# Column-normalised attention and a soft mixture of experts: two tiles of each unit split instead of three, five value halves loaded transposed, and a new order of steps and loads

## The chip, the core and the metric

The kernel runs on one NeuronCore of one Trainium2 chip. The metric is the device time of one execution in microseconds. Before the change it is 343.02 us (median of three runs, 342.92 to 343.14). The engines are named as the profile names them: PE (TensorE), DVE (VectorE), ACT (ScalarE), POOL (GpSimd) and SP (SyncE, which issues nearly all DMAs here).

## What is computed

Four batches of q, k and v, each 5056 tokens by 256 channels in fp32. The attention is between channels: a 256 by 256 matrix for each batch.

```python
qn = q / (norm(q, axis=1) + 1e-6);  kn = k / (norm(k, axis=1) + 1e-6)
s  = kn.transpose(0, 2, 1) @ qn / tau          # 256 x 256 per batch
a  = softmax(s, -1)
x  = (v @ a).reshape(4 * 5056, 256)
logits = x @ phi                               # 32 slots
d  = softmax(logits, 0);  slot_in = d.T @ x    # over all 20224 tokens
slot_out[e] = relu(slot_in[e] @ w1[e]) @ w2[e] # 8 experts, 4 slots each
out = softmax(logits, 1) @ slot_out
```

## The kernel before

**Stage one: 40 units.** Tokens of q and k come in units of 512 (four tiles of 128); ten units make a batch (`UB`), so units 0 to 39. `load_qk` brings one unit into a `raw` buffer (four of them, 1 MB each). `score_tiles` adds each tile's part of k-transposed times q to two banks of the accumulator memory, one for each half `m` of k's channels. A tile is treated in one of two ways. A **raw** tile (line 213) is multiplied in plain fp32. A **split** tile (lines 224 and 227) is first divided into a rounded part by ACT (`cast`, line 155) and the remainder by DVE (`low`, line 163), both in the tile `hl`; then one matmul of 512 columns and one of 256 do the work in the rounded type. `n_split` says how many of a unit's four tiles are split: none in unit 0, two up to unit 11, three from unit 12 on. For the column norms ACT squares every unit (`square`, line 181) and DVE adds it up (`add`, lines 194 to 197).

**The border between two batches.** When a batch's last unit is done, `att_join` copies the upper halves of the two score banks to SBUF (ACT, `shi`, line 244) and adds the lower halves (DVE, `ssb`, line 246). The next batch overwrites these banks, so its first score matmul waits for `ssb`. Then come the norms: `att_sums` (PE, `n`, line 253), `att_copy` (ACT, `nsb`, line 264), `att_cols` (PE, `nn`, line 270), `att_pow` (DVE `rn`, then POOL, line 276), `att_norm` (ACT `dg`, line 288), `att_row` (PE, `rq`, line 294); then scaling, exponentials and turns down to the batch's small matrix `M` (`att_phi`, `att_m`).

**Pairs of v.** v comes in pairs of 1024 tokens, five to a batch, pairs 0 to 19. `load_v` brings a pair in natural order (six buffers). For the logits v is needed with channels on the partitions: the first channel half comes from DRAM already transposed (`load_vt`, `vt0`, 0.5 MB a pair), the second is transposed by PE (`turn`, `vTp`, line 368, four transposes for each half pair) and copied out by ACT (`turned`, line 385). `logits` (line 399) then multiplies by `M`; each two or three pairs make a group whose running maximum goes through DVE and two tiny matmuls (`peak_row`, `peak_run`, `shift`: `rp`, `rowrun`, `cp`); `gather` (PE, `G`, line 508) multiplies the exponentials by natural v and, with that, frees the pair's buffer.

**Order.** Nothing schedules this by itself. Each step is entered in a list with a number (`at(key, step, ...)`): unit `u` has the keys around `u`. The list is sorted and emitted, so each engine, SP's queue too, executes strictly in the order of the keys.

**Stage two.** A second list takes over behind unit 39. The unit buffers (`raw`, `hl`, `sq`) are given back and the same memory is cut into seven 1 MB slots `w` and six half MB slots `x`, for the last pairs of v and for the expert weights. In this list the last batch's small chain, the logits of pairs 15 to 19, the gathers 11 to 19 and the exponentials of `combine` (the softmax over slots: DVE `cm`, POOL and ACT `nat`) take turns. The first load in it is the second half of pair 16, whose first half the first list has put at its end; both go to the buffer that `gather` of pair 10 frees.

**Stage three.** The experts (`up`, `H`, line 901; `down`, `O`, line 927), then 20 output pairs (`out_pair`, line 992) of 1 MB each, written to DRAM.

Of the kernel before, what the change touches and what calls it, by code (L numbers as in the profile page):

```python
# [8 lines left out]
F32 = mybir.dt.float32  # L9
F32R = mybir.dt.float32r  # L10
# [13 lines left out]
def colnorm_attention_soft_moe(  # L24
# [9 lines left out]
    vt7: bass.AP,  # L34
    tau: bass.AP,
    phi: bass.AP,
    w1: bass.AP,
    w2: bass.AP,
    sel: bass.AP,
    oa: bass.AP,  # L40
# [50 lines left out]

    def load_vt(p, t=None, slot=None):
        b, i = divmod(p, PB)
        if slot:
            t = slot(f"vt{p}_0")
        if t is None:
            t = tpool.tile([P, 8 * P], F32, tag="vt0", name=f"vt{p}_0", bufs=3)
        if i < PB - 1:
            sp.dma_start(t, vt8[b, i])
        else:  # L100
            sp.dma_start(t[:, : 8 * P - HD], vt7[b])
        vts[p, 0] = t

# [17 lines left out]
    act.activation(warm, ones[:, 0:1], AF.Exp)  # L121
    phi_sb = const.tile([P, 2, S], F32, name="phi_sb")
    rtau = const.tile([P, 1], F32, name="rtau")
    sel_sb = const.tile([P, 2], F32, name="sel_sb")
    act.dma_start(phi_sb, phi.rearrange("(n p) s -> p n s", p=P))
    act.dma_start(rtau, tau.partition_broadcast(P))
    act.dma_start(sel_sb, sel)
    fold = const.tile([P, S], F32, name="fold")
# [150 lines left out]
    def att_norm(b):  # L279
        rn = st[b]["rn"]  # L280
        dve.tensor_scalar_add(rn, rn, 1e-6)
        dve.reciprocal(rn, rn)
        rk = bpool.tile([P, 2], F32, tag="rk", name=f"rk{b}")
        dg = bpool.tile([P, C], F32, tag="dg", name=f"dg{b}")
        if b == 0:
            dve.reciprocal(rtau, rtau)
# [85 lines left out]
    def turned(i, m=1, where=None, eng=None):  # L372
        p, h = divmod(i, 2)
        if h == 0:
            if where:
                where = xslot(f"vt{p}_{m}")
            else:
                where = tpool.tile([P, 8 * P], F32, tag="vt1", name=f"vt{p}_{m}", bufs=2)
            vts[p, m] = where
        x = vts[p, m]  # L380
        tp, n = tps[i, m]
        if eng is dve:
            dve.tensor_copy(x[:, h * UT : h * UT + n], tp[:, :n])
        else:
            act.copy(x[:, h * UT : h * UT + n], tp[:, :n])  # L385
# [233 lines left out]
    for b in range(3):  # L619
        k = UB * (b + 1)  # L620
        at(k - 0.42, att_join, b)
        at(k + 0.20, att_sums, b)
        at(k + 0.45, att_copy, b)
        at(k + 0.55, att_cols, b)
# [165 lines left out]
    at(0.6, last_exp, 0)  # L790
# [297 lines left out]
```

## Time and profile before

| what | value |
|---|---|
| median of three runs | 343.02 us |
| the profiled execution | 344.6 us |
| its span, first to last instruction | 342.8 us |
| PE busy | 278.7 us, 81% |
| DVE busy | 237.5 us, 69% |
| ACT busy | 208.3 us, 61% |
| DMA traffic | 110.36 MB, 322 GB/s on average |

The profile is of one execution. A group's line gives its count, its busy time in us and the mean of one instruction in ns. A row of the timeline gives start and duration in us and, in square brackets, how long the engine stood idle before it and for whom. A row of a stretch gives its length, then the busy time of PE, of PE's weight loads, of DVE, ACT and POOL (with instruction counts), the granted clock of PE as a share of full speed, the busy share of the DMA engines and their GB/s. PE rows overlap: the time between two starts, not the duration of one, is what a matmul costs.

### The profile page before, as it was taken

The page shows a single profiled execution, that of the slowest core. Times are in us where ns is not written, and L with a number is a line of the kernel's source. Part 1 is how long each engine was busy: PE and PEld are TensorE (multiplying, and loading weights), DVE is VectorE, ACT ScalarE, POOL GpSimd, SP SyncE. Part 2 cuts the span into 40 slices and gives each one's busy share as a digit, 9 for nine tenths or more (in the row PEclk, how much of TensorE's full clock was granted, in tenths as well). Part 3 has the DMA queues.
Part 4 walks back from the last instruction along what each step waited for, and adds up shares of the span by engine and source line. Part 5 has one row for each costly group of instructions (what it writes and reads, how often), then busy time and mean ns, then how long its engine had stood idle before and what let it go on. Part 6 is the DMA issues. An engine that isn't in the chain of part 4 may idle for free. (4 is left out here: it accounts for less than half of the span.)

```text
span 342.8 us, 5518 instructions
## 1 busy us (share of the span) xinstructions
PE 278.7 (81%) x2164; PEld 194.1 (57%) x2164; DVE 237.5 (69%) x340; ACT 208.3 (61%) x281; POOL 27.8 (8%) x18
## 2 busy tenths in 40 slices
PE   4899869899799899999989998839689998898000
PEld 2687638677566778667667675514345355565000
DVE  1399955799996889987879994526755245999000
ACT  1978865799795898787788863514530235677000
POOL 0000002000002000002000001021303231200000
PEclk9999969999999999999999999958785899999655
DMA  5999998799866889987897940999999602999997
GB/s 186 424 382 302 422 414 350 284 354 367 358 228 227 344 302 395 358 306 267 318 386 294 326 168 10 380 399 415 422 413 416 234 2 94 419 402 401 420 403 283
DMA packets 21401, 110.36 MB, mean 322 GB/s; under 512 B 2944, under 2 KB 3200, under 8 KB 12800
## 3 DMA queue, kind: packets, MB, share of 16 engines
q1 hardware_dynamic: 20816, 109.98, 82.9%
q8 instruction: 17, 0.28, 0.3%
q10 hardware_dynamic: 560, 0.03, 0.1%
q14 instruction: 8, 0.07, 0.0%
HBM read 89.29 MB, written 20.71 MB: 321 GB/s over the span
## 5 line engine op out<-in xcount | busy, mean ns | idle before, releaser
L224 PE MATMUL S<-hl 128*128 128x512 f32 x212 | 83.7, 429 | 3.4 <-DVE ssb L246 3.1
L181 ACT ACTIVATE sq<-raw 128x2048 f32<-128x2048 f32 x36 | 69.0, 1916 | 13.9 <-DMA raw<-in_qk_dram 6.6
L163 DVE TENSOR_TENSOR hl<-raw,hl 128x1536 fp32r<-128x1536 f32 (+1 forms) x39 | 62.5, 1603 | 19.2 <-ACT hl L155 18.9
L197 DVE TENSOR_TENSOR sq<-sq,sq 128x2048 f32<-128x2048 f32 (+1 forms) x37 | 73.4, 1983 | 0.0
L213 PE MATMUL S<-raw 128*128 128x256 f32 (+1 forms) x216 | 57.7, 400 | 5.2 <-DMA raw<-in_qk_dram 5.2
L155 ACT CAST hl<-raw 128x1536 fp32r<-128x1536 f32 (+1 forms) x39 | 52.7, 1352 | 13.9 <-issue 8.8
L227 PE MATMUL S<-hl 128*128 128x256 f32 x212 | 59.6, 281 | 0.0
L224 PEld LDWEIGHTS S<-hl 128*128 128x128 f32 x212 | 40.0, 189 | 24.3 <-issue 10.4
L213 PEld LDWEIGHTS S<-raw 128*128 128x128 f32 (+1 forms) x216 | 39.6, 199 | 12.4 <-DMA raw<-in_qk_dram 7.0
L227 PEld LDWEIGHTS S<-hl 128*128 128x128 f32 x212 | 40.3, 190 | 0.4
L385 ACT COPY vt<-vTp 128x512 f32<-128x512 f32 (+1 forms) x40 | 22.9, 582 | 18.3 <-PE vTp L368 18.0
L368 PE MATMUL vTp<-ident,v 128*128 128x128 f32 (+1 forms) x160 | 25.0, 281 | 6.8 <-DMA v<-in_v_dram 6.8
L992 PE MATMUL op<-so,cT 32*128 32x256 f32 x320 | 27.7, 410 | 2.9 <-DVE o L987 1.5
L399 PE MATMUL L<-vt,M 128*32 128x256 f32 (+1 forms) x320 | 25.2, 432 | 2.8 <-ACT M L356 1.3
L985 ACT COPY o<-op 128x512 f32<-128x512 f32 x40 | 21.2, 598 | 8.7 <-PE op L992 5.8
L992 PEld LDWEIGHTS op<-so,cT 32*128 32x128 f32 x320 | 19.7, 183 | 11.0 <-DVE o L987 6.3
L987 DVE COPY o<-op 128x512 f32<-128x512 f32 x40 | 24.2, 672 | 2.4 <-PE op L992 2.4
L508 PE MATMUL G<-v,dn 128*32 128x256 f32 (+1 forms) x320 | 25.3, 400 | 0.0
L276 POOL TENSOR_TENSOR rn<-rn,half 128x4 f32<-128x4 f32 x4 | 8.4, 2107 | 203.3 <-DVE rn L275 102.2
L368 PEld LDWEIGHTS vTp<-ident,v 128*128 128x128 f32 (+1 forms) x160 | 18.5, 142 | 10.9 <-issue 10.0
L399 PEld LDWEIGHTS L<-vt,M 128*32 128x32 f32 x320 | 9.2, 120 | 14.5 <-issue 6.3
L508 PEld LDWEIGHTS G<-v,dn 128*32 128x32 f32 (+1 forms) x320 | 11.8, 114 | 8.8 <-issue 3.9
(124 smaller groups left out, 253.1 us busy)
## 6 DMA issues: line engine op xcount, KB each, us to landing
raw<-in_qk_dram SPq DMA_DIRECT2D x35, 1024.0 KB, 6.4
out_dram<-o SPq DMA_DIRECT2D x16, 1024.0 KB, 11.7
v<-in_v_dram SPq DMA_DIRECT2D x31, 512.0 KB, 6.9
w<-in_moe_w_dram SPq DMA_DIRECT2D x14, 1024.0 KB, 12.4
vt<-in_vt_dram SPq DMA_DIRECT2D x16, 512.0 KB, 8.2
raw<-in_qk_dram SPq DMA_DIRECT2D x4, 768.0 KB, 6.0
out_dram<-o SPq DMA_DIRECT2D x4, 768.0 KB, 13.7
v<-in_v_dram SPq DMA_DIRECT2D x2, 1024.0 KB, 10.3
```

Of the source, the lines that this page charges most:

```text
L155: act.copy(hl[:, :ns, 0::2, :], raws[u][:, :ns])
L163: dve.tensor_tensor(hl[:, :ns, 1::2, :], raws[u][:, :ns], hl[:, :ns, 0::2, :].bitcast(F32), op=ALU.subtract)
L181: act.activation(sq, raws[u], AF.Square)
L197: dve.tensor_tensor(a[:, lo:hi], a[:, lo:hi], s[:, lo:hi], op=ALU.add)
L213: pe.matmul(sm[:, :C], raw[:pc, j, 1, cols], raw[:pc, j, 0, :], start=st[b]["open"][m], stop=False, skip_group_check=True,)
L224: pe.matmul(sm, hl[:, j, 2, cols], rhs, start=st[b]["open"][m], stop=False, skip_group_check=True)
L227: pe.matmul(sm[:, :C], hl[:, j, 3, cols], hl[:, j, 0, :], start=False, stop=last, skip_group_check=True)
L368: pe.transpose(tp[:, n : n + pc], vs[p][:pc, 4 * h + jj, P * m : P * m + P], ident[:pc, :pc])
L399: pe.matmul(L[S * g : S * g + S, :n, :], M[:, m, :], x[:, :n, S * g : S * g + S], start=m == 0, stop=m == 1,)
L508: pe.matmul(gp[S * g : S * g + S, :C], dn[:pc, x, j, :], vt[:pc, j, :], start=x == 0 and j < G, stop=x == n - 1 and j >= G,)
L987: dve.tensor_copy(dst, src)
L992: pe.matmul(ops[g][:, h, :], cT[b][S * g : S * g + S, 4 * i : 4 * i + 4, :].rearrange("s j t -> s (j t)"), so[S * g : S * g + S, :], start ...
```

## The change

Five things change, and nothing else.

1. `n_split` is two for every unit but the first. From unit 12 on, one tile in four goes from the split to the raw way. The `hl` tile holds two tiles instead of three and has three buffers instead of two.
2. The second channel half of v is loaded transposed from DRAM for pairs 0, 3, 6, 9 and 12 (`turned_pairs`), as one more `load_vt` behind the first; `turn` and `turned` of these pairs go away (ten half pairs, 40 transposes of PE, ten copies of ACT).
3. At the first unit of a batch, `raw` tiles come ahead of the split ones; `att_join` moves a quarter of a unit earlier, and DVE's `low` of that unit moves behind it; `att_sums`, `att_copy` and `att_cols` move later.
4. The loads of stage two have a new order: pairs 18 and 19 and the weights of experts 0 and 1 first, then the transposed halves of 18 and 19, then pair 16 (now wholly in stage two), pair 17 and the rest. The seven 1 MB slots have two names, four `w` and three `y`.
5. `phi`, `tau` and a small selector are packed into one array, `few`, loaded once by SP ahead of unit 8, in place of three loads that ACT issued at the start.

```diff
 def n_split(u):
-    return 0 if u == 0 else 2 if u < UB + 2 else 3
+    return 2 if u else 0
...
-    hl = apool.tile([P, 3, 4, C], F32R, tag="hl", name=f"hl{u}", bufs=2)
+    hl = apool.tile([P, 2, 4, C], F32R, tag="hl", name=f"hl{u}", bufs=3)
...
-    at(u - 0.95, low, u)
+    at(u - (0.62 if first else 0.95), low, u)
...
-    raw_at = u + 0.5 if first and u else u - (0.30 if u % 2 or u < FV else 0.04) if u else -0.6
+    raw_at = u if first and u else u - (0.30 if u % 2 or u < FV else 0.04) if u else -0.6
...
+turned_pairs = set(range(0, 14, 3))
 for i in range(29):
+    if i // 2 in turned_pairs:
+        continue
...
-    at(k - 0.42, att_join, b)
+    at(k - 0.67, att_join, b)
...
-for p in range(17):
+for p in range(16):
...
             at(k + h + 0.996, load_vt, p)
+            if p in turned_pairs:
+                at(k + h + 0.997, load_vt, p, 1)
+at(3.5, lambda: sp.dma_start(few_sb, few))
```

On VectorE at the border from batch 0 to batch 1, these rows stand one behind the other before (`hl10` is the remainder of unit 10, `ssb0` the joined scores of batch 0 from the banks `S0_0` and `S0_1`, `sq0` the sum of squares):

```order
L197 TENSOR_TENSOR sq0_129<-sq0_129,sq8_293 128x2048
L163 TENSOR_TENSOR hl10_324<-raw10_257,hl10_324 128x4x256
L246 TENSOR_TENSOR ssb0_341<-shi0_342,S0_0_131 128x256
L246 TENSOR_TENSOR ssb0_341<-shi0_342,S0_1_132 128x256
L194 TENSOR_TENSOR sq0_129<-sq0_129,sq9_316 128x1536
L195 TENSOR_TENSOR sq0_129<-sq0_129,sq9_316 64x512
```

And in the changed kernel:

```order
L191 TENSOR_TENSOR sq0_125<-sq0_125,sq8_292 128x2048
L240 TENSOR_TENSOR ssb0_337<-shi0_338,S0_0_127 128x256
L240 TENSOR_TENSOR ssb0_337<-shi0_338,S0_1_128 128x256
L157 TENSOR_TENSOR hl10_323<-raw10_254,hl10_323 128x4x256
L188 TENSOR_TENSOR sq0_125<-sq0_125,sq9_315 128x1536
L189 TENSOR_TENSOR sq0_125<-sq0_125,sq9_315 64x512
```

The remainder of unit 10 has moved behind the joined scores. On ACT the square of unit 10, which stood ahead of the two copies `shi0`, now stands behind them. On PE the order there was: half of unit 10's split tiles, `n0`, the other half, the raw tiles, `nn0`, the raw tiles of unit 11. It is now: the raw tiles of unit 10, its split tiles, `n0`, the raw tiles of unit 11, `nn0`.

In SP's queue, between stage one and stage two, these loads follow each other before (`v16` is pair 16 in natural order, `vt16_0` its transposed first half, `w1_0` the first weights of expert 0; the names in brackets are the engines and DMAs whose progress SP waits for):

```order
L86 DMA v15_1735<-in_v8_dram 128x1024 [waits DMAHW1_49,PE_49]
L86 DMA v15_1735<-in_v8_dram 128x1024 [waits DMAHW2_49]
L99 DMA vt15_0_1784<-in_vt8_dram 128x1024 [waits DMAHW3_49]
L86 DMA v16_1858<-in_v8_dram 128x1024 [waits DMAHW4_49,PE_49]
L86 DMA v16_1858<-in_v8_dram 128x1024 [waits DMAHW5_49]
L99 DMA vt16_0_1875<-in_vt8_dram 128x1024 [waits DMAHW6_49]
L86 DMA v18_1877<-in_v8_dram 128x2048 [waits DMAHW7_49,DVE_49,Activation_49]
L99 DMA vt18_0_1887<-in_vt8_dram 128x1024 [waits DMAHW0_49,DVE_49]
L101 DMA vt19_0_1889<-in_vt7_dram 128x960 [waits DMAHW1_49,DVE_49]
L86 DMA v17_1891<-in_v8_dram 128x2048 [waits DMAHW2_49,PE_49]
L99 DMA vt17_0_1906<-in_vt8_dram 128x1024 [waits DMAHW3_49,PE_49]
```

And in the changed kernel:

```order
L95 DMA vt15_0_1674<-in_vt8_dram 128x1024 [waits DMAHW6_49]
L84 DMA v18_1758<-in_v8_dram 128x2048 [waits DMAHW7_49,DVE_49,Activation_49]
L86 DMA v19_1760<-in_v7_dram 128x1792 [waits DMAHW0_49,DVE_49,Activation_49]
L88 DMA v19_1760<-in_vh_dram 64x256 [waits DMAHW1_49]
L705 DMA w1_0_1763<-in_moe_w1_dram 128x2048 [waits DVE_49,DMAHW2_49,PE_49,Activation_49]
L705 DMA w1_1_1765<-in_moe_w1_dram 128x2048 [waits DVE_49,DMAHW3_49,PE_49,Activation_49]
L95 DMA vt18_0_1767<-in_vt8_dram 128x1024 [waits DMAHW4_49,DVE_49]
L97 DMA vt19_0_1769<-in_vt7_dram 128x960 [waits DMAHW5_49,PE_49]
L84 DMA v16_1771<-in_v8_dram 128x2048 [waits DMAHW6_49,PE_49]
L95 DMA vt16_0_1773<-in_vt8_dram 128x1024 [waits DMAHW7_49]
L84 DMA v17_1783<-in_v8_dram 128x2048 [waits DMAHW0_49,PE_49]
L95 DMA vt17_0_1798<-in_vt8_dram 128x1024 [waits DMAHW1_49,PE_49]
```

Pair 16, which stood at the head with its wait for PE's gather of pair 10, now stands behind pairs 18 and 19, two expert weights and two transposed halves. Pair 18 goes to the buffer of unit 36 and waits for ACT and DVE alone; pair 19 follows into the buffer of unit 37; `w1_0` and `w1_1` go to the buffers of units 38 and 39 and wait for PE's, ACT's and DVE's last use of them.

More of the change, by code (lines that the diff above doesn't have):

```diff
@@ L34, in colnorm_attention_soft_moe @@
     vt7: bass.AP,
-    tau: bass.AP,
-    phi: bass.AP,
+    few: bass.AP,
     w1: bass.AP,
     w2: bass.AP,
-    sel: bass.AP,
     oa: bass.AP,
@@ L90, in load_v, with load_vt @@
                 sp.dma_start(vt[:HD, 7], vh[b])
-    def load_vt(p, t=None, slot=None):
+    def load_vt(p, m=0, t=None):
         b, i = divmod(p, PB)
-        if slot:
-            t = slot(f"vt{p}_0")
         if t is None:
-            t = tpool.tile([P, 8 * P], F32, tag="vt0", name=f"vt{p}_0", bufs=3)
+            t = tpool.tile([P, 8 * P], F32, tag=f"vt{m}", name=f"vt{p}_{m}", bufs=3)
         if i < PB - 1:
-            sp.dma_start(t, vt8[b, i])
+            sp.dma_start(t, vt8[b, i, m])
         else:
-            sp.dma_start(t[:, : 8 * P - HD], vt7[b])
-        vts[p, 0] = t
+            sp.dma_start(t[:, : 8 * P - HD], vt7[b, m])
+        vts[p, m] = t
     load_qk(0, ((0, 1), (1, 2), (2, 4)))
@@ L121, in colnorm_attention_soft_moe @@
     act.activation(warm, ones[:, 0:1], AF.Exp)
-    phi_sb = const.tile([P, 2, S], F32, name="phi_sb")
+    few_sb = const.tile([P, 2 * S + 3], F32, name="few_sb")
+    phi_sb = few_sb[:, : 2 * S].rearrange("p (n s) -> p n s", n=2)
+    sel_sb = few_sb[:, 2 * S : 2 * S + 2]
     rtau = const.tile([P, 1], F32, name="rtau")
[L124 to L127, printed above, removed]
     fold = const.tile([P, S], F32, name="fold")
@@ L285, in att_norm @@
         if b == 0:
-            dve.reciprocal(rtau, rtau)
+            dve.reciprocal(rtau, few_sb[:, 2 * S + 2 :])
         for i in range(2):
@@ L377, in turned @@
             else:
-                where = tpool.tile([P, 8 * P], F32, tag="vt1", name=f"vt{p}_{m}", bufs=2)
+                where = tpool.tile([P, 8 * P], F32, tag="vt1", name=f"vt{p}_{m}", bufs=3)
             vts[p, m] = where
@@ L620, in colnorm_attention_soft_moe @@
         k = UB * (b + 1)
-        at(k - 0.42, att_join, b)
-        at(k + 0.20, att_sums, b)
-        at(k + 0.45, att_copy, b)
-        at(k + 0.55, att_cols, b)
+        at(k - 0.67, att_join, b)
+        at(k + 0.47, att_sums, b)
+        at(k + 0.60, att_copy, b)
+        at(k + 0.75, att_cols, b)
         at(k + 0.95, att_pow, b)
@@ L684, in colnorm_attention_soft_moe @@
     wpool = ctx.enter_context(tc.tile_pool(name="wpool", bufs=1, reuse_waits="tile"))
+    nw = [0]
     def wslot(name):
-        return wpool.tile([P, 8, C], F32, tag="w", name=name, bufs=7)
+        i = nw[0] % 7
+        nw[0] += 1
+        tag, n = ("w", 4) if i < 4 else ("y", 3)
+        return wpool.tile([P, 8, C], F32, tag=tag, name=name, bufs=n)
     def xslot(name):
@@ L716, in load_vw, with load_vx @@
         load_v(p)
+    def load_vx(p):
+        load_vt(p, 0, xslot(f"vt{p}_0"))
     def last_be():
@@ L778, in colnorm_attention_soft_moe @@
     plan.clear()
-    at(0.0, load_v, 16, (1,))
-    at(0.0, load_vt, 16)
-    at(0.1, load_vw, 18)
+    for p in (18, 19):
+        at(0.0, load_vw, p)
+    for e in (0, 1):
+        at(0.0, load_w1, e, wslot)
+    for p in (18, 19):
+        at(0.01, load_vx, p)
+    at(0.02, load_v, 16)
+    at(0.02, load_vt, 16)
     at(0.3, gather, 11)
-    at(0.31, load_vt, 18, None, xslot)
-    at(0.31, load_vt, 19, None, xslot)
     at(0.31, load_v, 17)
@@ L788, in colnorm_attention_soft_moe @@
     at(0.55, load_vt, 17)
-    at(0.56, load_vw, 19)
     at(0.6, last_exp, 0)
@@ L875, in colnorm_attention_soft_moe @@
     for t, e, slot in (
-        (0.6, 0, wslot), (0.6, 1, wslot), (0.6, 2, wslot), (0.6, 3, wslot), (0.6, 4, wslot),
+        (0.6, 2, wslot), (0.6, 3, wslot), (0.6, 4, wslot),
         (7.2, 5, vslot), (10.1, 6, vslot), (11.1, 7, vslot),
@@ L896, in up @@
         if len(hss) == r:
-            hss.append(tpool.tile([P, F], F32, tag="vt1", name=f"hs{r}", bufs=2))
+            hss.append(tpool.tile([P, F], F32, tag="vt1", name=f"hs{r}", bufs=3))
         hp = bank(hb[r, x], f"H{r}_{x}")
@@ L1050 @@
     add("vh", v[:, n4 + n7 :])
-    add("vt8", v[:, :n4, :P].reshape(B, 4, 2 * UT, P).transpose(0, 1, 3, 2))
-    add("vt7", v[:, n4:, :P].transpose(0, 2, 1))
-    add("tau", np.asarray(inputs["tau"]).reshape(1))
-    for name in ("moe_phi", "moe_w1", "moe_w2"):
-        add(name, inputs[name])
+    add("vt8", v[:, :n4].reshape(B, 4, 2 * UT, 2, P).transpose(0, 1, 3, 4, 2))
+    add("vt7", v[:, n4:].reshape(B, N - n4, 2, P).transpose(0, 2, 3, 1))
     sel = np.zeros((4, 32, 2), np.float32)
@@ L1060 @@
             sel[g, 4 * e : 4 * e + 4, r] = 1.0
-    add("sel", sel.reshape(128, 2))
+    phi = np.asarray(inputs["moe_phi"]).reshape(2, P, S).transpose(1, 0, 2).reshape(P, 2 * S)
+    tau = np.broadcast_to(np.asarray(inputs["tau"], np.float32).reshape(1, 1), (P, 1))
+    add("few", np.concatenate([phi, sel.reshape(P, 2), tau], axis=1))
+    for name in ("moe_w1", "moe_w2"):
+        add(name, inputs[name])
     flat = nc.dram_tensor("out_0_dram", (B * N * C,), F32, kind="ExternalOutput").ap()
```

## The prediction

> **What bounds the kernel now.** I read the stretches first. Columns: length, busy time of PE, its weight loads, DVE, ACT, POOL, granted clock, DMA share, GB/s.
>
> ```profile
> 68.00:205.00 137.00, 130.16 (x965) 97.08 (x964) 123.25 (x153) 113.13 (x134) 4.92 (x2) 1.00 0.84 314
> 215.00:260.00 45.00, 32.48 (x316) 17.79 (x315) 24.35 (x64) 16.30 (x44) 8.35 (x4) 0.79 1.01 409
> 300.00:343.00 43.00, 15.54 (x178) 10.85 (x174) 17.52 (x27) 12.87 (x24) 0.00 (x0) 0.72 0.95 380
> ```
>
> From unit 13 on, stage one belongs to PE: it stands idle 6.84 of 137 us at full clock. DVE is close behind (123.25 of 137, 90%). Stage two is different: PE idles 12.5 of 45 us while the DMAs are full. The output at the end runs at the DMAs' rate, so what comes earlier ahead of it moves the end by as much.
>
> Where PE waits, its timeline shows. First the border from batch 0 to batch 1, then a stretch with its clock:
>
> ```profile
> 41.32 0.28 PE L227 MATMUL S<-hl 128*128 128x256 f32 x1
> 44.67 0.50 PE L224 MATMUL S<-hl 128*128 128x512 f32 x1 [3.07 <-DVE ssb L246]
> 46.67 2.51 PE L253 MATMUL n<-sq,ones 128*32 128x512 f32 x8 [1.03 <-DVE sq L194]
> 53.48 0.95 PE L270 MATMUL nn<-pick,nsb 128*128 128x1 f32 x8
> 58.47 0.70 PE L294 MATMUL rq<-dg,ones 128*128 128x256 f32 x2
> 67.28 0.51 PE L224 MATMUL S<-hl 128*128 128x512 f32 x1
> ```
> ```profile
> 46.00:48.00 2.00, 1.33 (x7) 0.38 (x8) 2.00 (x3) 0.70 (x1) 0.00 (x0) 0.53 1.05 422
> ```
>
> Unit 9 ends at 41.60; PE waits 3.07 us for the joined scores and 1.03 us for the squares, and then works at half clock for some six microseconds.
>
> Second, the way into stage two, PE's timeline and SP's:
>
> ```profile
> 208.80 1.07 PE L253 MATMUL n<-sq,ones 128*32 128x512 f32 x8
> 211.65 1.07 PE L508 MATMUL G<-v,dn 128*32 128x256 f32 x16
> 214.89 1.07 PE L508 MATMUL G<-v,dn 128*32 128x256 f32 x16
> 221.50 0.38 PE L456 MATMUL cp<-negone,rowrun 1*128 1x1 f32 x2
> 228.66 1.09 PE L368 MATMUL vTp<-ident,v 128*128 128x128 f32 x4 [6.79 <-DMA v<-in_v_dram]
> 236.67 0.64 PE L399 MATMUL L<-vt,M 128*32 128x256 f32 x8 [0.56 <-ACT vt L385]
> 243.40 0.35 PE L456 MATMUL cp<-negone,rowrun 1*128 1x1 f32 x2 [2.34 <-DVE rowrun L452]
> ```
> ```profile
> 196.15 0.43 SPq L99 DMA_DIRECT2D vt<-in_vt_dram  x1
> 212.78 0.80 SPq L86 DMA_DIRECT2D v<-in_v_dram  x2
> 216.02 0.33 SPq L86 DMA_DIRECT2D v<-in_v_dram  x1
> ```
>
> SP issues nothing between 196.58 and 212.78: the load of pair 16 is at its head and needs the buffer that the gather at 211.65 frees. Behind it everything else starts at once, and pair 17 (issued at 216.02) reaches PE only at 228.66, 6.79 us late.
>
> **The change part by part.**
>
> *The border to batch 1.* DVE's and ACT's rows there:
>
> ```profile
> 39.61 2.29 DVE L197 TENSOR_TENSOR sq<-sq,sq 128x2048 f32<-128x2048 f32 x1
> 41.81 1.22 DVE L163 TENSOR_TENSOR hl<-raw,hl 128x1024 fp32r<-128x1024 f32 x1
> 44.19 0.75 DVE L246 TENSOR_TENSOR ssb<-shi,S 128x256 f32<-128x256 f32 x2 [1.16 <-ACT shi L244]
> 44.86 1.75 DVE L194 TENSOR_TENSOR sq<-sq,sq 128x1536 f32<-128x1536 f32 x1
> 46.53 0.68 DVE L195 TENSOR_TENSOR sq<-sq,sq 64x512 f32<-64x512 f32 x1
> ```
> ```profile
> 43.81 0.63 ACT L244 COPY shi<-S 128x256 f32<-128x256 f32 x2
> 47.30 1.91 ACT L181 ACTIVATE sq<-raw 128x2048 f32<-128x2048 f32 x1 [1.92 <-DVE sq L195]
> 49.21 0.59 ACT L264 COPY nsb<-n 128x512 f32<-128x512 f32 x1
> ```
>
> Today the copies `shi` start at 43.81 because a square stands ahead of them, and PE starts 0.86 us later. In the new order nothing stands ahead, so they start at 41.60 and PE's raw tiles of unit 10 at 42.46 (DVE's addition is over at 41.90). What a tile costs on PE, pieces of the chain of waits give (start, us, and the four rows of one tile or one turn together, or one row):
>
> ```profile
> 179.75 0.86 PE S L213 x4
> 180.97 0.23 PE S L224
> 181.19 0.12 PE S L227
> 182.70 0.44 PE vTp L368 x4
> ```
>
> A raw tile is 0.86 us, a split one 2 x (0.23 + 0.12) = 0.70, four transposes 0.44. So unit 10 takes 1.72 + 1.40 and ends at 45.58. DVE joins until 41.60 + 1.13 = 42.73 (today 43.81 to 44.94), does `low` until 43.95 and the last addition (2.35, from 44.86 to 47.21) until 46.30; there `n` starts, takes 1.07 (the row at 208.80, full clock), and unit 11's raw tiles bring PE to 49.09. ACT's square and `nsb` are done by 46.30 + 1.91 + 0.59 = 48.80, in time for `nn`. From `nn` to `rq` DVE, POOL and ACT set the pace: 58.47 - 53.48 = 4.99, which I keep. `rq` comes at 54.08, 4.4 us earlier. The 8.8 us from `rq` to unit 13's split tiles (67.28) are a chain too and stay; at their end PE has one raw tile more behind it and two split tiles ahead instead of three, 0.70. **Together -5.1.** Ends: -5.7, if the full clock shortens `nn` as well, and -2, if the clock falls anyway (below).
>
> *Units 14 to 39.* Each has 0.86 - 0.70 = 0.16 more on PE: 26 x 0.16 = +4.2. Pairs 3, 6, 9 and 12 lose 8 x 0.44 = -3.5. (Pair 0's two turns lay in the chain just counted.) ACT and DVE gain much more than that, but they are not the bound. Of PE's small waits there, one kind is covered by the longer raw tiles:
>
> ```profile
> PE Mp L343 <- ACT aT L335: 1.1, 2, 0.5
> ```
>
> This -1.1 I take. At five ends of groups a split tile (0.70) no longer stands between `rp` and `cp`: between 0 and +3.5; I take 0, since the shorter `low` lets DVE reach the maxima about half a microsecond sooner. **Sum -0.4, from -2 to +3.5.**
>
> *The transposed loads.* Five times 0.5 MB on queues that have room (share 0.84) except around the first border. At 409 GB/s one takes 1.28 us. The waits of all engines for the unit buffers, by releaser, stand against a cost:
>
> ```profile
>   DMA raw<-in_qk_dram: 19.3, 9
> ```
>
> The nine waits lie in the kernel's first microseconds; PE's list of waits from 68 to 205, from which the row on `Mp` comes, names no DMA. **0, at most +6.4.**
>
> *The load order of stage two.* SP now meets pair 18 right behind 196.58, with waits for ACT and DVE on unit 36 only, then pair 19, two weights and two halves, 5 MB or 12.8 us at 409 GB/s. They follow the release of the last four unit buffers and are over at about 212 to 214, when today's stream begins. Pair 16 is asked for at 212.78 as today, pair 17 behind the gather at 214.89; 1 + 0.5 + 1 MB take 6.4 us: pair 17 lands at about 221, and PE asks for it at 221.88. So the wait of 6.79 goes. What is next late:
>
> ```profile
> 225.63 2.34 POOL L767 TENSOR_TENSOR nat<-nat,cm 128x1280 f32<-128x1280 f32 x1 [12.56 <-DVE cm L766]
> ```
> ```profile
> 234.87 1.27 ACT L771 ACTIVATE nat<-nat 128x1280 f32<-128x1280 f32 x1
> 236.04 1.06 ACT L385 COPY vt<-vTp 128x512 f32<-128x512 f32 x2
> ```
> ```profile
> 240.82 2.43 DVE L452 TENSOR_TENSOR rowrun<-rowrun,row 1x128 f32<-1x128 f32 x1
> ```
>
> ACT's `nat` needs POOL's, which ends at 227.97 and does not move with the loads. ACT then does `nat` from 227.97 instead of 234.87, and the copy `vt` behind it, on which PE's logits at 236.67 wait, 6.9 us earlier. A PE at full clock would only wait longer there; the chain behind it (DVE, POOL, `rowrun`, `cp`) is the same as today. From the turn of pair 17 to `nat` it takes 6.2 us today (228.66 to 234.87); from 221.88 that gives 228.1, so the turn is in time even at today's pace. **-6.8, ends -6.9 and 0.**
>
> *The clock.* Rows first:
>
> ```profile
> 214.00:216.00 2.00, 1.70 (x18) 0.71 (x18) 1.79 (x7) 0.75 (x4) 0.00 (x0) 1.00 0.87 256
> 244.00:246.00 2.00, 2.00 (x16) 1.44 (x17) 0.52 (x2) 1.44 (x6) 0.00 (x0) 0.53 1.06 434
> ```
>
> After the idle 2.34 us before 243.40 the clock is at 0.53; in the stretch from 214 it stays at 1.00. The new border has waits of about 0.9, 0.7 and, at unit 12, two near 1.5 us; I take full clock. [...]
>
> *The packed small load and the start:* 34 KB, once, no one near it: 0, to -0.2.
>
> **Sum.** -5.1 - 0.4 - 6.8 = -12.3 against the profiled execution's own 344.6 us: 332.3. The median of the runs, 343.02, lies 1.6 below that, so the forecast is 330.7; its own range is 327 to 334.
>
> **The rivals.**
>
> *Raw units come late at the first border* (chance 0.14). The DMAs are full there (1.05 in the stretch from 46), and PE now wants its units five microseconds sooner while two more halves are in the queue. Price: 2 to 5 x 1.28, so 333.3 to 337.1. For it: the full queue. Against: no wait of PE for `raw` behind the start.
>
> *Pair 17 is still late* (0.12). SP's queue is strict, and pair 16 stands behind loads that need units 38 and 39 finished. If these six start only at the end of unit 39, 12.8 us of them lie ahead of pair 16 and the stall stays: 330.7 + 6.8 = 337.5. It decides where the last of the six lands behind about 217. Against: four of the six need buffers released from 196 on.
>
> *The clock falls at unit 12* (0.09): some six microseconds at half clock, +3, so 333.7.
>
> *Slower: the DMAs are the bound of stage one* (0.06). If the 314 GB/s of the long stretch is all that the stream gives there, 2.6 MB more take 8.3 us, the border's gain ends as a wait for the next unit, and only stage two's is left: 343.0 + 8.3 - 6.8 = 344.5. It begins where a unit lands after ACT could have begun its `cast`. Against: 409 to 422 GB/s in the rows at 46 and 215.
>
> That the change doesn't do what it says is excluded by the order of the instructions.
>
> **How the numbers follow.** Forecast 0.57, the rivals 0.14, 0.12, 0.09 and 0.06, and 0.02 for a mixture of them near no change. The first four are all faster: 0.92. No change within 0.2% (0.7 us, about what a measurement of this kernel can tell): 0.02. Slower: 0.06. The range, 327 to 337, holds the forecast's own, the clock and nearly all late units, and leaves out the late pair 17 and the slower case, 0.20.
>
> **What the changed profile would show.** Right: PE's wait for `ssb` at the border near 1 us and full clock there; unit 13 about 5 us earlier, unit 39 about 5.5; DMA share near full between 190 and 210; no wait for pair 17, and in its place one of about 3 us for the `vt` copy behind `nat`. Wrong: waits of PE or ACT for `raw` behind unit 4; `cp` waits grown by more than 0.5 us each; a wait for pair 16 or 17; the clock at half in stage one.

## The result, and the profile after

The changed kernel takes **327.42 us** (median of four runs, 326.09 to 329.03), 343.08 for the kernel before on the same chip: a ratio of 0.954, 95% interval 0.948 to 0.960. The forecast was 330.7, the range 327 to 337. The profiled execution takes 326.35 us (span 324.6). That is at the low end of the changed kernel's runs, and the 344.6 of the profile before is at the high end of its own, so the two profiles lie 18.25 us apart and the medians 15.7. Medians are of all executions of a kernel; a ratio leaves out those that took over 1.5% longer than the fastest of the same kernel.

First two stretches of the changed kernel, with the columns as before: the first border and the long stretch of stage one.

```profile
42.00:54.00 12.00, 10.94 (x59) 8.02 (x57) 8.27 (x13) 7.78 (x9) 1.94 (x1) 1.00 1.02 414
68.00:193.00 125.00, 119.80 (x877) 89.89 (x870) 100.47 (x145) 91.60 (x118) 3.86 (x2) 1.00 0.94 350
```

The same two before:

```profile
42.00:54.00 12.00, 8.30 (x30) 5.15 (x30) 5.18 (x6) 9.04 (x8) 0.00 (x0) 0.72 1.02 413
68.00:193.00 125.00, 118.53 (x886) 88.99 (x888) 111.69 (x134) 104.35 (x123) 4.92 (x2) 1.00 0.86 323
```

The border now runs at full clock (1.00, 0.72 before), and in the long stretch VectorE is busy 80% of the time instead of 89. Next PE's rows of the border:

```profile
40.14 1.99 PE L207 MATMUL S<-raw 128*128 128x256 f32 x8 [0.78 <-DVE ssb L240]
46.67 0.95 PE L264 MATMUL nn<-pick,nsb 128*128 128x1 f32 x8
51.11 0.70 PE L288 MATMUL rq<-dg,ones 128*128 128x256 f32 x2 [0.26 <-ACT dg L282]
58.92 1.07 PE L393 MATMUL L<-vt,M 128*32 128x256 f32 x16 [0.43 <-ACT M L350]
```

The wait for the joined scores is 0.78 us instead of 3.07, and `rq` comes at 51.11 instead of 58.47. Unit 9 ended at 40.14 - 0.78 = 39.36 (41.60 before), so 2.2 of these 7.36 us were won ahead of the border and 5.1 at it.

Then PE's waits in stage one between 58 and 196 us, and the three rows of the list before (66 to 210 us) that are gone:

```profile
PE rq L288 <- ACT dg L282: 1.7, 2, 0.9
PE L L393 <- ACT M L350: 1.6, 3, 0.7
PE cp L450 <- DVE rowrun L444: 1.2, 1, 1.2
PE L L393 <- DVE L L388: 0.7, 2, 0.3
PE cp L450 <- DVE rowrun L446: 0.4, 2, 0.2
```
```profile
PE rp L441 <- DVE mx L436: 1.5, 1, 1.5
PE Mp L343 <- ACT aT L335: 1.1, 2, 0.5
PE L L399 <- ACT vt L385: 0.3, 1, 0.3
```

A row gives what PE waited for, the sum in us, how often, and the longest. Some waits have grown: `cp` for `rowrun` (line 444) has 1.2 instead of 0.7, and 0.7 of waiting for DVE's `L` is new.

Last, three of PE's waits in stage two, with what stands behind two of them on ACT and DVE:

```profile
213.03 0.63 PE L362 MATMUL vTp<-ident,v 128*128 128x128 f32 x4 [1.13 <-DMA v<-in_v_dram]
219.84 0.64 PE L393 MATMUL L<-vt,M 128*32 128x256 f32 x8 [1.86 <-ACT vt L379]
226.57 0.55 PE L450 MATMUL cp<-negone,rowrun 1*128 1x1 f32 x2 [2.35 <-DVE rowrun L446]
```
```profile
218.04 1.27 ACT L779 ACTIVATE nat<-nat 128x1280 f32<-128x1280 f32 x1 [1.21 <-POOL nat L775]
219.22 1.05 ACT L379 COPY vt<-vTp 128x512 f32<-128x512 f32 x2
```
```profile
223.99 2.43 DVE L446 TENSOR_TENSOR rowrun<-rowrun,row 1x128 f32<-1x128 f32 x1
```

Pair 17 is awaited for 1.13 us instead of 6.79, and 1.86 us of waiting for the copy `vt` behind ACT's `nat` have come up. Where the 18.25 us lie, cut at the same PE rows of both traces (L0, L13, L15: first logits of pairs 0, 13, 15; so L3 below):

| stretch | before | after | difference |
|---|---|---|---|
| start to the end of unit 9 | 41.60 | 39.36 | -2.2 |
| to the first `rq` | 16.87 | 11.75 | -5.1 |
| to L0 | 7.81 | 7.81 | 0 |
| to L13 | 143.41 | 139.88 | -3.5 |
| to L15 | 19.99 | 14.78 | -5.2 |
| to the `cp` at 226.57 | 13.72 | 12.98 | -0.7 |
| to the experts' first matmul | 21.07 | 19.74 | -1.3 |
| to the end | 78.35 | 78.26 | -0.1 |

### The profile page after: what moved, and what is told of

It reads as the page before. It is cut to its first block, busy times and chain, and to the rows that moved or that the text cites. A ratio compares the mean times of both kernels' runs of the same rounds, so it can differ in the third digit from the quotient of the medians.

```text
span 324.6 us, 5407 instructions
## 1 busy us (share of the span) xinstructions
PE 269.2 (83%) x2124; PEld 191.2 (59%) x2124; DVE 222.7 (69%) x340; ACT 191.8 (59%) x271; POOL 26.2 (8%) x18
## 3 DMA queue, kind: packets, MB, share of 16 engines
q1 hardware_dynamic: 21536, 112.60, 89.7%
## 4 chain that ended last, share of the span: by engine, by line
PE 53%; DVE 11%; issue 4%; ACT 3%; DMA 2%; POOL 1%; DVEq 0%; ACTq 0%
PE S L207 14%; PE S L218 8%; PE L L393 5%; PE G L502 5%; PE op L1002 4%; PE vTp L362 4%; PE S L221 3%; PE H L911 3%; DVE o L997 3%; PE O L937 2%; DMA v<-in_v_dram 2%; DVE cT L971 1%; ACT lt L472 1%; DVE sq L191 1%; PE n L247 1%
## 5 line engine op out<-in xcount | busy, mean ns | idle before, releaser
L207 PE MATMUL S<-raw 128*128 128x256 f32 (+1 forms) x328 | 80.2, 388 | 4.8 <-DMA raw<-in_qk_dram 4.1
L207 PEld LDWEIGHTS S<-raw 128*128 128x128 f32 (+1 forms) x328 | 59.9, 193 | 16.9 <-DMA raw<-in_qk_dram 4.2
L218 PE MATMUL S<-hl 128*128 128x512 f32 x156 | 61.7, 430 | 0.3 <-DVE hl L157 0.3
L157 DVE TENSOR_TENSOR hl<-raw,hl 128x1024 fp32r<-128x1024 f32 x39 | 47.5, 1218 | 19.0 <-ACT hl L149 18.9
L221 PE MATMUL S<-hl 128*128 128x256 f32 x156 | 43.6, 280 | 0.0
L149 ACT CAST hl<-raw 128x1024 fp32r<-128x1024 f32 x39 | 40.6, 1041 | 1.6 <-DMA raw<-in_qk_dram 1.5
L218 PEld LDWEIGHTS S<-hl 128*128 128x128 f32 x156 | 29.3, 188 | 13.9 <-issue 4.4
L379 ACT COPY vt<-vTp 128x512 f32<-128x512 f32 (+1 forms) x30 | 17.3, 580 | 21.3 <-PE vTp L362 21.3
L221 PEld LDWEIGHTS S<-hl 128*128 128x128 f32 x156 | 29.5, 189 | 0.4
L362 PE MATMUL vTp<-ident,v 128*128 128x128 f32 x120 | 19.2, 283 | 1.6 <-DMA v<-in_v_dram 1.6
L362 PEld LDWEIGHTS vTp<-ident,v 128*128 128x128 f32 x120 | 13.7, 142 | 6.1 <-issue 3.2
```

The lines of the kernel that those rows point to most:

```text
L157: dve.tensor_tensor(hl[:, :ns, 1::2, :], raws[u][:, :ns], hl[:, :ns, 0::2, :].bitcast(F32), op=ALU.subtract)
L207: pe.matmul(sm[:, :C], raw[:pc, j, 1, cols], raw[:pc, j, 0, :], start=st[b]["open"][m], stop=False, skip_group_check=True,)
L218: pe.matmul(sm, hl[:, j, 2, cols], rhs, start=st[b]["open"][m], stop=False, skip_group_check=True)
L221: pe.matmul(sm[:, :C], hl[:, j, 3, cols], hl[:, j, 0, :], start=False, stop=last, skip_group_check=True)
L362: pe.transpose(tp[:, n : n + pc], vs[p][:pc, 4 * h + jj, P * m : P * m + P], ident[:pc, :pc])
```

## The experiments

The first four do one part of the change alone; the next four take a part back or move a suspected wait; the last four ask which engine paid, and measure the changed kernel once more. A ratio is to the kernel before on the same chip, whose median there was 344.1 to 344.4 us, with its 95% interval.

**The packed small load alone.**

```diff
-act.dma_start(phi_sb, phi.rearrange("(n p) s -> p n s", p=P))
-act.dma_start(rtau, tau.partition_broadcast(P))
-act.dma_start(sel_sb, sel)
...
+at(3.5, lambda: sp.dma_start(few_sb, few))
```

> Before, with the packed small load alone (one load by SyncE ahead of unit 8 in place of three that ScalarE issued at the start). Theory: the three small loads, 560 packets of under 512 bytes, hold up the first units (the second part of unit 0 landed at 6.18 us in the trace of before and at 5.18 in that of after, the later units 2.2 us apart), and TensorE follows the units there; so unit 9 ends about 2.2 us earlier and the whole execution takes about 341 us, 2 less. Rival, the prediction's own term: nothing to 0.2 us, 343; the earlier start of after then comes from another part, or is lost at the border again because the norms there do not come sooner.

342.12 us, ratio 0.994 (0.991 to 0.997). The loads of the first units, issue to landing in us at the end of each row: first before, then this kernel.

```profile
raw<-in_qk_dram SPq DMA_DIRECT2D x4, 1024.0 KB, 10.2
raw<-in_qk_dram SPq DMA_DIRECT2D x1, 512.0 KB, 7.1
```
```profile
raw<-in_qk_dram SPq DMA_DIRECT2D x5, 1024.0 KB, 7.0
raw<-in_qk_dram SPq DMA_DIRECT2D x1, 512.0 KB, 4.9
```

Unit 9 ends at 39.45, 2.15 us sooner, as the theory had it. But the wait for the joined scores is 3.07 us here as well, and what was won at the start is partly lost in unit 17 (below). Later runs made the cause doubtful.

**The order of late loads alone** (the lines of stage two as in the change).

```diff
-for p in range(17):
+for p in range(16):
...
-at(0.0, load_v, 16, (1,))
+for p in (18, 19):
+    at(0.0, load_vw, p)
...
```

> Before, with the new load order of stage two alone. Theory: the wait of 6.79 us for pair 17 goes, the chain over POOL's and ScalarE's nat and the copy vt sets the pace instead, and about 6.8 us are won: 336.3 us, TensorE's cp of the fourth batch's first group 6.8 us sooner than in before (243.40). Rival: pair 17 stays late, because pair 16 still waits for the gather and the six loads ahead of it for units 38 and 39: 343, with a wait of more than 5 us for v of pair 17.

336.94 us, ratio 0.977 (0.971 to 0.982); without one execution of 341.64 the median is 335.96, 8.2 us less. PE has no wait for `v` at all in stage two; two of its waits there:

```profile
231.75 0.94 PE L399 MATMUL L<-vt,M 128*32 128x256 f32 x8 [3.02 <-ACT vt L385]
238.48 0.35 PE L456 MATMUL cp<-negone,rowrun 1*128 1x1 f32 x2 [0.66 <-DVE rowrun L452]
```

The new wait of 3.02 us for `vt` is the one that the prediction named, with its size. So the theory holds for the waits, but not for the time of `cp`, which comes 4.9 us sooner (238.48, 243.40 before) and not 6.8. Another 3.8 us are won between that `cp` and the experts: the granted clock is 1.00 there from 238 to 246, and 0.51 from 244 to 250 in the kernel before, behind its wait of 2.34 us for `rowrun`.

**The new order at the borders alone.**

```diff
-raw_at = u + 0.5 if first and u else ...
+raw_at = u if first and u else ...
...
-at(k - 0.42, att_join, b)
+at(k - (0.67 if b == 0 else 0.64), att_join, b)
...
```

> Before, with the new order at the batch borders alone (at the second and third border three split tiles still stand, and the joins there come at 0.64 instead of 0.67). Theory: the wait for the joined scores falls from 3.07 to about 1 us, TensorE keeps the full clock and the small chain up to rq starts about 4.4 us sooner: 338.5 to 339.5 us. Rival: the border only moves the wait to the norms (n waits for the last addition of squares, which DVE ends when it did) or a raw unit comes late, and 1 to 2 us are left: 341 to 342.

339.66 us, ratio 0.986 (0.981 to 0.991), 4.5 us less. Its stretch at the border, and the row of the wait:

```profile
42.00:54.00 12.00, 10.34 (x54) 7.76 (x55) 8.31 (x12) 9.31 (x9) 2.50 (x1) 1.00 1.03 418
```
```profile
41.99 1.99 PE L213 MATMUL S<-raw 128*128 128x256 f32 x8 [0.77 <-DVE ssb L246]
```

Full clock and a wait of 0.77: the theory holds, and the DMA queue, as full as before (1.03 and 1.02), holds nothing up.

**Two split tiles and the loaded halves alone** (with a third buffer for the second halves, which the change has too).

```diff
-return 0 if u == 0 else 2 if u < UB + 2 else 3
+return 2 if u else 0
...
+                    if p in turned_pairs:
+                        at(k + h + 0.997, load_vt, p, 1)
...
```

> Before, with two split tiles in every unit and the five turned pairs loaded, and nothing else. Theory after the traces: TensorE's waits for DVE and ScalarE in units 14 to 39 shrink, because each unit gives VectorE and ScalarE less to do, and 2 to 3 us are won: 340 to 341 us. Rival one, the prediction's sum: TensorE is the bound, 4.2 more for raw tiles and 3.5 less for turns, with the 1.1 of Mp: 342.6 and no change that counts. Rival two: the 2.6 MB more of loads hold up the units, 345 to 350, with waits for raw behind unit 4.

337.19 us, ratio 0.979 (0.975 to 0.983): 7.0 us less, more than any theory had. In the trace L0 to L13 is 3.9 us shorter, rather over the 2 to 3 expected; 2.0 more lie between L13 and the fourth batch's first `cp`, where the wait for pair 17 is 5.53 instead of 6.79, and 0.9 at `rq` to L0. No wait for `raw` stands behind unit 4. The prediction's sum is refuted, and so is the rival of the loads, in this kernel.

The four alone win 2.05 + 8.2 + 4.5 + 7.0 = 21.8 us, the whole change 16.2 on its second measurement below. By the traces two parts meet at the wait for pair 17 (between L13 and that `cp` 5.7 and 2.0 us alone, 5.9 in all), and three of them each shorten the stretch from that `cp` to the experts (3.8, 0.9 and 1.0), which the whole shortens by 1.3. What else overlaps was not separated.

**Three split tiles again, the rest as changed** (but for two `hl` buffers of three tiles and the joins of the new borders alone).

```diff
-return 2 if u else 0
+return 0 if u == 0 else 2 if u < UB + 2 else 3
```

> The changed kernel with three split tiles again from unit 12 on (two hl buffers of three tiles), all else as changed. Theory: fewer split tiles pay because VectorE and ScalarE have less to do in each unit, which takes the waits ahead of rp and cp away; with three of them the wait of about 1.5 us for mx in unit 17 comes back, and two or three at the other groups' ends, which outweighs the 0.16 us a unit that TensorE would win: 328 to 331 us. Rival, TensorE's sum alone: 26 x 0.16 = 4.2 us less, 323 us.

332.15 us (331.95 without one execution of 337.15), ratio 0.965 (0.956 to 0.975). L0 to L13 is 143.95 us instead of 139.88. Its waits of PE (some of the rows):

```profile
PE cp L450 <- DVE rowrun L446: 1.5, 2, 0.8
PE rp L435 <- DVE mx L430: 1.4, 1, 1.4
PE Mp L337 <- ACT aT L329: 1.1, 2, 0.5
```

The wait for `mx` is back, as the theory said. PE's waits of over 0.1 us between L0 and L13 add up to 8.97 us, to 5.19 in the changed kernel. Not all of the 4.1 us are waits, though: the clock is at 0.50 from 62 to 65 in this trace, where three split tiles take 3.55 us, 2.27 elsewhere. The time lies 1 us above the theory's span; by the trace 1.5 us were lost at the start, not in the units. TensorE's sum alone is refuted.

**All pairs turned again, the rest as changed.**

```diff
-turned_pairs = set(range(0, 14, 3))
+turned_pairs = set()
```

> The changed kernel with all pairs turned by TensorE again (no second half of v loaded transposed), all else as changed. Theory: ten half pairs, 40 transposes of TensorE at 0.11 and ten copies of ScalarE at 0.59 come back; TensorE's 4.4 us are paid in full in stage one, 331.5 to 332.5 us. Rival one: the DMA queues (share 0.95 from 56 to 196 us in the trace of after, 0.84 before) are close to a bound, and 2.6 MB less give most of it back: 327 to 329. Rival two: ScalarE's copies make further waits, more than 334.

330.79 us, ratio 0.961 (0.950 to 0.973): between the theory and rival one. The trace decides: L0 to L13 is 143.29, 3.4 us more, and the 32 transposes in it take 3.7 us. The DMA share falls from 0.94 to 0.88 and nothing is given back for that.

```profile
68.00:193.00 125.00, 120.11 (x896) 90.87 (x889) 98.41 (x141) 92.20 (x121) 3.85 (x2) 1.00 0.88 318
```

**Packed, but at the old time.**

```diff
-act.dma_start(phi_sb, phi.rearrange("(n p) s -> p n s", p=P))
-act.dma_start(rtau, tau.partition_broadcast(P))
-act.dma_start(sel_sb, sel)
+act.dma_start(few_sb, few)
...
```

> Before with phi, tau and the selector packed into one array, but still loaded by ScalarE at the start (128 packets instead of 560, at the old time). Theory one, the number of packets: the first units land nearly as early as in the trace of after (second part of unit 0 within 0.4 us of 5.18, the later ones 0.5 us late at most), unit 9 ends at 39.4 to 39.9 instead of 41.60, and about 2 us are won, 342. Theory two, the place in time: any load beside the first units holds them up for its own fixed time, unit 9 ends after 41, and the time stays at that of before.

343.24 us, ratio 0.996 (0.993 to 1.000). Unit 9 ends at 39.57, as theory one had it; the time is one us less, not two.

**Steps of the output weights moved.**

```diff
-at(8.1, combine, 0, 1)
+at(8.9, combine, 0, 1)
...
-at(10.5, combine, 1, 0)
-at(13.8, combine, 1, 1)
-at(17.0, combine, 1, 2)
```

The three steps of batch 1 stand among the experts' `up` instead.

> The changed kernel with the exponentials of the first batch's output weights (ScalarE's nat) behind the two copies vt of pair 17 instead of ahead of them, and all three steps of the second batch's output weights moved from stage two to the time of the experts. Theory: what follows the stall for pair 17 is no longer a load but this chain; TensorE's wait of 1.86 us for vt goes, and rowrun, no longer beside a long POOL operation, takes 0.28 instead of 2.43 us, so cp of the fourth batch's first group comes 3.5 to 5 us sooner: 323 to 324.5 us. Rival: the late loads set the end of stage two (the gathers of pairs 18 and 19 or the experts' first weights), and less than 1 us is left: 326.5 to 327.5.

325.71 us, ratio 0.949 (0.940 to 0.957); 1.2 above the theory's span. The wait for `vt` is gone, but `cp` comes at 224.97 instead of 226.57, 1.6 us sooner and not 3.5 to 5, since PE waits 1.08 us for the maximum ahead of it, and `rowrun` again stands beside a POOL operation (the last step of batch 0):

```profile
223.45 1.38 DVE L446 TENSOR_TENSOR rowrun<-rowrun,row 1x128 f32<-1x128 f32 x1
```

**That step moved as well** (the edit against the changed kernel).

```diff
-at(8.1, combine, 0, 1)
-at(9.5, combine, 0, 2)
...
+at(8.9, combine, 0, 1)
...
+combine(0, 2)
 combine(2, 0)
+combine(1, 0)
 flip_h(0)
...
+combine(1, 1)
 combine(2, 1)
 flip_h(1)
+combine(1, 2)
 combine(2, 2)
```

> The changed kernel with the first batch's nat behind the copies of pair 17, and the last step of the first and all three steps of the second batch's output weights moved to the time of the experts. In the run before this one, rowrun still stood beside a POOL operation (1.38 us instead of 0.28) and the maximum of pair 17 behind DVE's cm of the first batch. Theory: both go, cp of the fourth batch's first group comes 2 to 2.5 us sooner than there (224.97), and the profiled time falls from 324.99 to between 322.5 and 323.5. Rival: TensorE's queue or the late loads take it back, and it stays within 0.5 us of 324.99.

**321.60 us, ratio 0.933 (0.929 to 0.938)**, 321.08 us without one execution of 324.83, better than both kernels: the changed kernel has 327.89 beside it. DVE's and PE's rows:

```profile
221.66 0.28 DVE L446 TENSOR_TENSOR rowrun<-rowrun,row 1x128 f32<-1x128 f32 x1
```
```profile
222.08 0.35 PE L450 MATMUL cp<-negone,rowrun 1*128 1x1 f32 x2 [0.19 <-DVE rowrun L446]
```

Away from POOL, `rowrun` takes 0.28 us, and `cp` comes 2.9 us sooner than in the run before. The profiled time, 320.46, is lower than the theory had: the stretch from that `cp` to the experts is also 2.8 us shorter than in the changed kernel's first trace, while what follows gives back 1.3. The clock behind `cp` is full in this run and at half in the changed kernel, behind its wait of 2.35 us for `rowrun`:

```profile
222.00:229.00 7.00, 5.17 (x62) 3.12 (x63) 3.95 (x15) 3.46 (x12) 0.00 (x0) 1.00 1.01 416
```
```profile
226.00:232.00 6.00, 4.97 (x34) 2.95 (x38) 3.31 (x13) 2.85 (x11) 0.28 (x1) 0.50 0.97 348
```

**VectorE's load back, the changed kernel else.** One tile's remainder is computed twice.

```diff
+        if u >= UB + 2:
+            dve.tensor_tensor(
+                hl[:, :1, 1::2, :], raws[u][:, :1], hl[:, :1, 0::2, :].bitcast(F32), op=ALU.subtract
+            )
```

> The changed kernel with one tile's remainder computed twice by VectorE in every unit from 12 on: VectorE has about 0.6 us more in each of 28 units, nearly what a third split tile cost it, and TensorE and ScalarE have the same work as in the changed kernel. Theory: it was VectorE's load that made TensorE wait ahead of rp and cp, so waits of 3 to 4 us come back in all (about 1.4 for mx in unit 17): 329.5 to 331.5 us by the changed kernel's 327.4. Rival: VectorE is not what paid, and the time stays within 1 us of the changed kernel's.

**ScalarE's load back, the changed kernel else.**

```diff
+        if u >= UB + 2:
+            act.copy(hl[:, :1, 0::2, :], raws[u][:, :1])
```

> The changed kernel with one tile's rounded part copied twice by ScalarE in every unit from 12 on: ScalarE has about 0.6 us more in each of 28 units, VectorE and TensorE the same work as in the changed kernel. Theory (VectorE is what paid): within 1 us of the changed kernel's 327.4. Rival: the cast of ScalarE, on which VectorE's remainder waits, makes the same waits of 3 to 4 us: 329.5 to 331.5.

**The changed kernel once more.**

> The changed kernel once more, as the measure for the three kernels beside it: 326 to 329 us, 0.95 to 0.96 of before. By the idea that an equal wait can halve TensorE's clock in one execution and not in another, its runs lie at two or more times about 2 us apart, without any difference in the program.

VectorE's load: 336.88 us, with two executions at 331.58 and 332.63 and four from 336.39 to 337.49, ratio 0.970 (0.963 to 0.977). ScalarE's load: 328.15, ratio 0.954 (0.949 to 0.958). The changed kernel: 327.89, ratio 0.953 (0.948 to 0.957); its ten executions in all lie from 326.09 to 330.69, and not in groups 2 us apart, as the idea had it. The added operations between 60 and 215 us, VectorE's and ScalarE's, a kernel each (count, busy us, mean ns):

```profile
L161 DVE TENSOR_TENSOR hl<-raw,hl 128x512 fp32r<-128x512 f32 x26 | 18.0, 692 | 0.9
```
```profile
L151 ACT CAST hl<-raw 128x512 fp32r<-128x512 f32 x26 | 16.1, 619 | 0.8
```

PE's waits for DVE in stage one, with VectorE's load:

```profile
PE cp L454 <- DVE rowrun L450: 2.2, 2, 1.1
PE rp L439 <- DVE mx L434: 1.7, 1, 1.7
PE cp L454 <- DVE rowrun L448: 1.6, 1, 1.6
```

with ScalarE's:

```profile
PE cp L452 <- DVE rowrun L446: 1.6, 1, 1.6
PE rp L437 <- DVE mx L432: 0.4, 1, 0.4
PE cp L452 <- DVE rowrun L448: 0.4, 2, 0.2
```

and with neither, in the second trace of the changed kernel:

```profile
PE cp L450 <- DVE rowrun L444: 1.6, 1, 1.6
PE rp L435 <- DVE mx L430: 0.5, 1, 0.5
PE cp L450 <- DVE rowrun L446: 0.4, 2, 0.2
```

VectorE's load brings 3.0 us of these waits back. All its executions lie above all ten of the changed kernel, 3.7 us above its median at the least and about 9 in four of six, which is more than the theory's 2 to 4. ScalarE's load costs 0.3 us by the medians; its trace has the waits of this second trace, and 0.8 us more of them than the first. So VectorE is what paid most. The trace with VectorE's load is of one of the longer executions: it is 6.4 us longer than the second trace of the changed kernel. Of these, 4.7 lie between L0 and L13: PE's waits of over 0.1 us there are 9.4 instead of 6.1, and most of the rest is the clock, which is at half (0.50) from 82.9 to 89.7 us instead of 82.9 to 86.3. Between `rq` of the fourth batch and L15 stand 1.4 more. How this divides in the shorter executions is not shown.

## Why the prediction was right or wrong

**The border: right, with some luck in the figure** (-5.1 forecast, -5.1 measured; alone -4.5). `ssb` was awaited for 0.78 us where 0.86 was worked out, and the full clock, which the sum took and a rival doubted, is there. All five traces with the old order at the border show a clock below full in the stretch from 42 to 54 (0.72 in four, 0.86 in the packed load at the old time), all nine with the new one 1.00. But of the -5.1 forecast only -4.4 were for `rq`; the other 0.7 were for unit 13's third split tile, which the stretches above count behind L0. The missing 0.7 came mainly from a term that was kept: from `nn` to `rq` the chain took 4.44 us (46.67 to 51.11), not the 4.99 of before. That the clock would be full was the author's choice: no run shows how long PE can stand idle without losing it. At unit 17 it fell to half behind waits of 1.45 and 0.72 us in the packed load alone, and stayed at 1.00 behind 1.47 and 0.71 in the kernel before.

**The load order of stage two: right** (-6.8; in the whole change -5.2 up to L15 and -0.7 more to the `cp`, alone -5.7 up to the `cp`). The detail was off: pair 17 is still late by 1.13 us, and the wait for `vt` is 1.86 instead of about 3. The two together are 2.99. The sum had the six loads ahead of pair 16 over when pair 16 is asked for. In the trace the last of them, `vt19_0`, is issued at 197.06 and lands 9.6 us later, at 206.7, though pair 16 was issued at 202.16; pair 17, issued at 205.41, takes 7.5 us. So the rival of the late pair 17 came true in small. Alone the wait for `vt` is 3.02 and none is left for pair 17.

**Units 14 to 39: the step that failed** (-0.4, with the 0.7 above -1.1; -3.5 between L0 and L13). The sum said that each unit has 0.16 more on PE, and that ACT and DVE "are not the bound". Both were off:

- A third split tile was priced at 0.70, a piece out of a run of them. Between L0 and L13, from the start of one group of PE rows to the next, the kernel before spends 63.4 us on 81 split tiles and 22.2 on 26 raw ones; the changed one 42.7 on 54 and 44.5 on 52. That is 0.78 and 0.79 for a split tile, since in 10 of 27 units the three stood in two runs (0.87 + 1.62 us instead of 2.27). So PE has 1.6 more, not 3.5 (the 4.2 less the 0.7 that were counted at the border). This is the term that was furthest off.
- The 32 transposes take 13.4 - 9.5 = 3.9, not 3.5.
- PE's waits of over 0.1 us fall from 6.8 to 5.2, by 1.6 instead of 1.1; the largest single one that went is the 1.5 for `mx`. The prediction has the maxima half a microsecond sooner there and counts the groups' ends as nothing.

1.6 - 3.9 - 1.6 = -3.9, and 0.4 us of small rows go the other way. In the second trace of the changed kernel L0 to L13 takes 142.6 us, 2.7 more than in the first, all of it ahead of L3, with the clock at half at unit 17 (0.50 from 83 to 86, last section), one of the prediction's signs of being wrong; the -3.5 compares two traces with full clock there.

The run with three tiles and the run with VectorE's load show what the relief of DVE is worth in the changed kernel. With three tiles PE's waits are 3.8 us more. Its time for the scores is 87.4 us instead of 87.2, of which 1.3 are the half clock from 62 to 65, so that the third split tile alone would save PE about 1.1. DVE, at 90%, was not the bound of the stage, but it was the bound at a few rows in each batch, and their waits count in full.

**The transposed loads at nothing: right on average, not in every execution.** PE has no wait for `raw` behind the start. ACT has, which the prediction names as a sign of being wrong: its casts wait for units that have not landed, here in the first and then in the second trace of the changed kernel.

```profile
79.73 1.04 ACT L149 CAST hl<-raw 128x1024 fp32r<-128x1024 f32 x1 [0.80 <-DMA raw<-in_qk_dram]
```
```profile
77.67 1.05 ACT L149 CAST hl<-raw 128x1024 fp32r<-128x1024 f32 x1 [1.33 <-DMA raw<-in_qk_dram]
82.93 1.04 ACT L149 CAST hl<-raw 128x1024 fp32r<-128x1024 f32 x1 [2.14 <-DMA raw<-in_qk_dram]
```

The mean share of 0.94 hides this: in the first trace the queue is full from 42 to 90 us (1.01 to 1.03 in stretches of 12 us) and at 0.85 from 90 to 120. There PE loses nothing by it: its one wait of over 0.1 us from L0 to L3 is 1.22 us, 1.21 in the run with two split tiles and loaded halves alone, whose casts wait for no unit there. In the second trace DVE's remainder waits 1.79 us for the first of the two late casts, and PE then 0.50 for `mx` and 1.61 for `rowrun`. With all pairs turned no cast waits for its unit at this place.

**The start at nothing: open** (-2.2 in the first pair of traces). The 560 packets of ScalarE's three loads looked like the cause, and the first two traces without them, of the changed kernel and of the packed load alone, did start sooner. But the second trace of the changed kernel has the late start as well, with the same program:

```profile
41.88 1.99 PE L207 MATMUL S<-raw 128*128 128x256 f32 x8 [0.77 <-DVE ssb L240]
```
```profile
raw<-in_qk_dram SPq DMA_DIRECT2D x5, 1024.0 KB, 8.7
raw<-in_qk_dram SPq DMA_DIRECT2D x1, 512.0 KB, 6.6
```

Unit 9 ends there at 41.1. In all, it ends at 41.0 to 41.6 in the four traces with the 560 packets; of the ten without them seven have 39.4 to 39.6 and three 40.9 to 41.1. So the late start does not need them. Whether they make it more frequent, these counts suggest and do not settle; the packed load alone is worth 1 to 2 us by its runs.

**From `cp` to the experts** 1.3 us went that no term named. The clock has a part in this stretch, as the late loads alone and the run with all steps moved show, and it varies between executions: the part of it from `slp` on is 7.5 us in the first trace of the changed kernel and 6.4 in the second.

By terms the prediction was 0.7 us short at the border, 2.4 in the units, 2.2 at the start and 1.3 ahead of the experts, and 0.9 too hopeful in stage two. That makes nearly all of the profiled difference, 18.25 instead of 12.3. It came within 3.3 us of the median, at the very edge of its range, because the second median keeps only 15.7 of it; that part is luck.

## What to carry to other kernels

Price an operation by the difference of two whole units in the trace, not by one piece of a run: three split tiles in two pieces took 0.87 + 1.62 us here, in one 2.27. Ask of an engine at 90% not whether it bounds the stage, but at which rows the bounding engine waits for it, and count every one of these rows. Where a load is taken off the path, look at once for long operations of other engines beside the small chain behind it: moving five of their steps was worth 6.3 us here, more than the border.

## What the runs showed of the hardware that was not expected

**A short VectorE operation stretched by GpSimd.** `rowrun`, 128 numbers from two SBUF inputs, takes 2.43 us beside POOL's `nat`, 1.38 beside another one and 0.28 with POOL idle, while DVE's maxima, which read PSUM, go through beside POOL at 0.39 to 0.42. In each of the 13 traces where it meets POOL it ends 0.14 or 0.15 us behind POOL's operation (243.25 behind 243.11 in the kernel before, 226.42 behind 226.28 in the changed one), so it takes as long as POOL still needs; with the late loads alone that is 0.75. What in POOL's operation holds it up these rows do not show; the run with all steps moved shows what it cost, 2.43 us against 0.28.

**The clock falls behind equal waits in some executions only.** At unit 17 PE's waits for `mx` and `rowrun` are 1.5 and 0.7 us in the traces of before and of the new borders alone, and the clock stays at 1.00; with the same two waits in the packed load alone and the late loads alone it is 0.51 to 0.52 in the three microseconds behind `cp`, and L0 to L3 takes 1.6 us more. One program did both, though behind unequal waits (1.2 us, and 0.5 and 1.6): the first and the second trace of the changed kernel there.

```profile
79.00:85.00 6.00, 5.19 (x25) 4.38 (x26) 5.97 (x8) 4.90 (x6) 0.00 (x0) 1.00 1.00 400
```
```profile
83.00:86.00 3.00, 3.00 (x8) 2.37 (x9) 2.59 (x4) 3.00 (x4) 0.00 (x0) 0.50 1.00 406
```

The longest single wait ahead of the second is 1.6 us. With three split tiles the clock falls at 61.7, and no wait of PE in the eight microseconds ahead of it is longer than 0.97. Read in steps of 1 us, the stretches at half clock in these traces last 3.4 us (82.9 to 86.3 in the second trace), 6.8 (225.6 to 232.5 in the first, 82.9 to 89.7 with VectorE's load) or 10.2 (257.8 to 268.0 in the kernel before), and the one that runs to the end 23.6 in the kernel before. Why the clock falls in one execution and not in another, these traces do not show. With the start, this makes a spread of some 4 us between executions of one program: 324.6 and 328.9 us of span for the changed kernel.
